# A new head: block 1's attention 8 half-slices earlier, raw weights in deeper flight, values loaded when a buffer is free

## The chip, the cores and the metric

The kernel runs on one core of one Trainium2 chip. The metric is the device time of that core in microseconds. Before the change the median of three runs is 1130.93 us (1129.2 to 1132.24).

The engines are named as the profile names them: PE is TensorE (PEld its weight loads), DVE is VectorE, ACT is ScalarE, POOL is GpSimd, and SP is SyncE, which here only issues DMAs. A q behind a name (SPq, ACTq) is that engine's sequencer.

## The reference

Three parts follow one another: windowed attention with sink tokens, a dense feed-forward layer with squared ReLU, and a mixture of eight experts of which each token takes one.

```python
# attention: q, k, v are (4, 8, 768, 64) float32; n_sink = 4, window = 128
scores = scale * np.matmul(q, k.transpose(0, 1, 3, 2))
keep = is_sink | in_window                 # key position < n_sink, or 0 <= row - key < window
scores = np.where(keep, scores, -1000000000.0)
a = softmax(scores)                        # with 1e-9 added to the sum
x = (a @ v) laid out as (3072 tokens, 512)
# dense layer: w_in (512, 2048), w_out (2048, 512), both float64
h = np.maximum(x @ w_in, 0.0);  x = (h * h @ w_out).astype(np.float32)
# experts: w_gate, w_output_gate (512, 8); w1 (8, 512, 1024); w2 (8, 1024, 512)
e_idx = argmax(x @ w_gate);  gate_w, eom = softmax weight, sigmoid of the output gate
out[token] = gate_w * eom * (np.maximum(x @ w1[e], 0.0) @ w2[e])
```

## The kernel before

The 3072 tokens are worked in 12 blocks of 256 (three to each of the four sequences). For a block t the attention makes its input x, then the dense layer runs over 16 units j of 128 hidden columns: `l1(t, j)` multiplies by a slice of w_in, applies ReLU and squares, and `l2` multiplies by a slice of w_out and adds up in PSUM, two units behind. The expert part comes after the twelfth block.

**Attention of a block.** Eight heads are taken as four pairs p, and a block's 256 rows as two halves n, which makes eight steps (p, n). `prep_k` and `prep_q` transpose k and q on TensorE; `scores` multiplies, applies the mask on VectorE (L528), exponentiates on ScalarE (L531) and normalises (L541, L543); `ptrans` transposes the probabilities (L560) and copies them (L564); `pv` multiplies by the values (L594) and copies out (L597). `attn_events` gives every such piece a due time in half-slices: a unit j of block t - 1 is two half-slices, and h0 is where block t's first scores are due. Events with a negative time lie in the head, ahead of the first unit of block 0. `loads` issues the DMAs of k, q and v for a block and a pair; `more`, called at the end of `prep_q`, loads two pairs ahead. Buffers are two for k and q, three for v.

**The weights.** w_in and w_out come as float64. They are converted on the chip in 32 pieces of 512 KB each, c = 2j for w_in's slice j and c = 2j + 1 for w_out's. `conv(c)` issues the raw load and returns `rest`, which does the work: two copies with a scale on ScalarE (L327, L330), two shift-and-or steps on VectorE (L334, L335) that give a float32 weight, and later `fin`, which splits it into a high part (L338, ScalarE) and a low part (L339, VectorE). Block 0 computes with the float32 weight itself, in TensorE's fp32 mode; all later blocks use the split parts. The first NBOOT = 3 raw pieces have buffers of their own (`braw`), the rest share three staging buffers (tag `stage`) with the set-up of the gate (`setup2`) and other short-lived tiles. `cstep(n)` does the next n pieces, with `fetch` loading ahead of them.

**What sets the order.** The program is written out by loops over half-slices: `for h in range(-46, 0)` is the head, with events, a conversion every third half-slice and the gate's set-up at h = -24; then come the units g = 16 t + j. A planner orders each engine's instructions ahead of the run from this written order, priorities (`tc.high_priority`) and estimated costs, and it may take an instruction early where its inputs and a buffer are there. `tc.keep_in_program_order` pins an instruction to the written order on its engine, and `behind(x, y)` puts x behind y on one engine without a semaphore. At run time every engine works in order, a DMA queue's issuing engine too, so a DMA that waits for a buffer holds what is behind it.

**Lines of the change.** The raw loads (L305 to L322), ScalarE's two copies (L327, L330), `loads` (L360), the q tiles (L439 to L443), `more` (L480), the end of `pv` (L596), `attn_events` (L647), the square in `l1` (L688), `cstep` (L897), the head (L919 to L948). `fill` (L105) puts small matmuls without a result between the head's others on TensorE.

Of the kernel before, what the change touches and what calls it, by code (L numbers as in the profile page):

```python
# [47 lines left out]
def kern(ctx, tc, q, k, v, n_sink, window, w_in, w_out, w_gate, w_og, w1, w2, out):  # L48
# [238 lines left out]

    fbuf = att.tile([128, 2, 512], F32, tag="PT", name="fbuf", bufs=1)

    fins, used = {}, {}  # L290

    def after(x, y):

# [11 lines left out]
    def conv(c):  # L305
        j, which = divmod(c, 2)
        if c < NBOOT:
            raw, dq = braw[c], A
        else:
            raw = cv.tile([128, 512, 2], I32, tag="stage", bufs=3, name="craw")  # L310
            dq = SY
        if which == 0:
            x = dq.dma_start(out=raw[:].rearrange("p (k f) w -> p k (f w)", k=4),
                         in_=w_in.bitcast(I32)[:, 256 * j:256 * j + 256].rearrange("(k p) f -> p k f", p=128))
            hi, lo = (WI[:, j, n].rearrange("p k f -> p (k f)") for n in range(2))
        else:
            x = dq.dma_start(out=raw[:].rearrange("p f w -> p (f w)"), in_=w_out.bitcast(I32)[128 * j:128 * j + 128, :])
            hi, lo = (WO[j // 8][:, j % 8, n] for n in range(2))
        if c < NBOOT + 2:
            tc.keep_in_program_order(x)  # L320
        if c < NBOOT:
            behind(x, brd[0])  # L322

        def rest():
            L, Hh = raw[:, :, 0], raw[:, :, 1]

            x = A.activation(out=Hh.bitcast(F32), in_=Hh.bitcast(F32), func=AF.Copy, scale=2.0 ** -112)  # L327
            if c < NBOOT:
                tc.keep_in_program_order(x)
            A.activation(out=L, in_=L.bitcast(U32), func=AF.Copy, scale=0.93 * 2.0 ** -29)  # L330
            n = NF * which + j
            f = fw[n] if n < len(fw) else fbuf[:, j % 2]
            fi = f.bitcast(I32)
            V.scalar_tensor_tensor(out=fi, in0=Hh, scalar=3, in1=L, op0=ALU.logical_shift_left, op1=ALU.bitwise_or)  # L334
            V.scalar_tensor_tensor(out=fi, in0=Hh, scalar=-2147483648, in1=fi, op0=ALU.bitwise_and, op1=ALU.bitwise_or)  # L335

            def fin():
                A.activation(out=hi, in_=f, func=AF.Copy)  # L338
                x = V.tensor_tensor(out=lo, in0=f, in1=hi.bitcast(F32), op=ALU.subtract)  # L339
                if n < len(fw):  # L340
                    after(x, used[n])

            if n < len(fw):
                fins[n] = fin
            else:
                fin()
        return rest
# [9 lines left out]
    moe.tile([128, HOME // 4], F32, name="gap1", bufs=1)  # L357
    xTs = {}

    def loads(t, p, kinds="kqvs"):  # L360
        b, u = divmod(t, NQ // 2)
        s0 = 256 * u
        for nm, src, m in (("k", k, 3), ("q", q, 2), ("v", v, 3)):
            if nm not in kinds:
                continue
            x = att.tile([128, m, 2, D], F32, tag=nm + "n", name=nm + "n", bufs=3 if nm == "v" else 2)
            lo = s0 - 128 * (m - 2)
            o = 0
            if lo < 0:
                lo, o = 0, 1  # L370
            nb = m - o
            for e in range(2):
                x_ = (A if t == 0 and (nm == "q" and p < 2 or nm == "v" and p == 0) else SY).dma_start(out=x[:, o:m, e, :],
                             in_=src[b, 2 * p + e, lo:lo + 128 * nb, :].rearrange("(n s) d -> s n d", s=128))
                if t == 0 and (p >= 2 or nm == "v"):
                    pin(x_)
                if brd and t == 0 and p < 3:
                    behind(x_, brd[0])
            nat[nm, t, p] = x
        if u == 0 and p == 0 and "s" in kinds:  # L380
            x = att.tile([H * NS, D], F32, tag="vs", name="vs", bufs=1)
            x_ = SY.dma_start(out=x[:], in_=v[b, :, 0:NS, :])
            if t == 0:
                pin(x_)
            nat["vs", b] = x
# [42 lines left out]
    def prep_q(t, p):  # L428
        x = nat.pop(("q", t, p))
        if t < T32:  # L430
            ps = psO.tile([128, 4, 128], F32, tag="O", name="psq")
        else:
            ps = psS.tile([128, 512], F32, tag="s0", name="psq")[:, 0:256].rearrange("p (n c) -> p n c", n=2)
        if t == 0:
            fill(ps[:].rearrange("p n c -> p (n c)"), 1)
        for n in range(2):
            PE.transpose(ps[:, n], x[:, n].rearrange("p h d -> p (h d)"), ident[:])
        if t < STK:
            own = t // T32  # L439
            if own not in qbuf:  # L440
                qbuf[own] = att.tile([128, 2, 2, 2, 128], F32R if own else F32, tag="qT", name=f"qT{own}", bufs=1)
            o = qbuf[own][:, p % 2]
            qTt[t, p] = o  # L443
        if t < T32:
            if p % 2:
                A.activation(out=o[:, 0], in_=ps[:, 0:2], func=AF.Copy)
            else:
                V.tensor_copy(out=o[:, 0], in_=ps[:, 0:2])
            Vt[t, p] = nat.pop(("v", t, p))
            more(t, p)  # L450
            return
        if t < STK:
            A.activation(out=o[:, 0], in_=ps[:, 0:2], func=AF.Copy)
            V.tensor_tensor(out=o[:, 1], in0=ps[:, 0:2], in1=o[:, 0].bitcast(F32), op=ALU.subtract)
        else:
            if "s" not in qbuf:
                o = qbuf["s"] = att.tile([128, 2, 2, 2, 128], F32R, tag="qT", name="qst", bufs=1)
                for e in range(2):
                    r = HALF[1 - e]
                    G.tensor_copy(out=o[r, 1, e].rearrange("p n (a c) -> p (n a) c", c=64),  # L460
                                  in_=ident[r, None, 64 * e:64 * e + 64].broadcast_to([64, 4, 64]))
            o = qbuf["s"]
            qTt[t, p] = o
            for e in range(2):
                A.activation(out=o[HALF[e], 0, e], in_=ps[HALF[e], 0:2], func=AF.Copy)
            for e in range(2):
                V.tensor_tensor(out=o[HALF[e], 1, e], in0=ps[HALF[e], 0:2], in1=o[HALF[e], 0, e].bitcast(F32), op=ALU.subtract)
            for e in range(2):
                G.tensor_copy(out=o[HALF[1 - e], 0, e], in_=o[HALF[e], 0, e].bitcast(F32))

        n0 = 1 if t % 3 == 0 else 0
        x = nat.pop(("v", t, p))
        o = att.tile([128, 3, 2, 2, D], F32R, tag="V", name="V", bufs=2)
        for e in range(2):
            G.tensor_copy(out=o[:, n0:3, e, e, :], in_=x[:, n0:3, e, :])
            G.tensor_tensor(out=o[:, n0:3, e, 1 - e, :], in0=x[:, n0:3, e, :], in1=o[:, n0:3, e, e, :].bitcast(F32), op=ALU.subtract)
        Vt[t, p] = o
        more(t, p)

    def more(t, p):  # L480
        tt, pp = (t, p + 2) if p + 2 < 4 else (t + 1, p - 2)
        if tt < NBLK:
            loads(tt, pp)

    def prep_sink(b):
        t = nat.pop(("vs", b))
# [14 lines left out]
    def scores(t, p, n):  # L501
# [26 lines left out]
                V.tensor_tensor_reduce(out=P[:, e, 0:W], in0=ps[e][:, 0:W], in1=mask[:, 0:W], scale=-SCALE, scalar=3.0e38,  # L528
                                       op0=ALU.add, op1=ALU.min, accum_out=st[:, e:e + 1])
        for e in range(2):  # L530
            A.activation(out=P[:, e, 0:W], in_=P[:, e, 0:W], func=AF.Exp, scale=-1.0, bias=st[:, e:e + 1],  # L531
                         accum_out=st[:, 4 + e:5 + e])
        V.tensor_scalar(out=st[:, 6:8], in0=st[:, 4:6], scalar1=1e-9, scalar2=None, op0=ALU.add)
        V.reciprocal(out=st[:, 6:8], in_=st[:, 6:8])  # L534
        if t >= T32 and i >= 2:
# [46 lines left out]
    def pv(t, p, n):  # L582
# [3 lines left out]
        if t < T32:  # L586
# [8 lines left out]
                              start=(kb == 0), stop=(kb == nk - 1))  # L595
            xo = xr if t else xT0  # L596
            A.activation(out=xo[:, p, 128 * n:128 * n + 128], in_=ps[:, 0:128], func=AF.Copy)  # L597
            return
        ps = psO.tile([128, 2, 2, 128], F32, tag="O", name="pso")
        for e in range(2):  # L600
# [46 lines left out]
    def attn_events(t):  # L647

        ev = []
        h0 = 32 * (t - 1) - 8  # L650
        a0, a1, a2, a3 = LEADS[min(t, 3)]
        for p in range(4):
            ev.append((h0 + 8 * p - a0, lambda p=p: prep_k(t, p)))
# [18 lines left out]
    def l1(t, j):  # L672
# [12 lines left out]
                PE.matmul(ps[:], lhsT=WI[:, j, a_, kk, :], rhs=x[:, b_, kk, :], start=(n == 0), stop=(n == 11))  # L685
        hq = moe.tile([128, 256], F32, tag="r", name="r", bufs=2)
        A.activation(out=hq[:], in_=ps[:], func=AF.Relu)  # L687
        E_ = G if t == 0 and j % 2 else V  # L688
        if t == 0 and NF + j < len(fw):
            o = moe.tile([128, 256], F32, tag="h2", name="h32", bufs=3, padded_shape=[128, 512])  # L690
            E_.tensor_tensor(out=o[:], in0=hq[:], in1=hq[:], op=ALU.mult)
# [205 lines left out]
    def cstep(n):  # L897
        for _ in range(n):
            if st_["done"] >= NC:
                return  # L900
            fetch(min(NC, st_["done"] + 2))
            rests.pop(st_["done"])()
            st_["done"] += 1

# [16 lines left out]
    loads(0, 2, "q")  # L921
    loads(0, 1, "v")
    loads(0, 0, "s")
    fetch(NBOOT)
    events = sorted((e for t in range(NBLK) for e in attn_events(t)), key=lambda e: e[0])
    events.reverse()

    def run_to(h):
        while events and events[-1][0] <= h:
            h_, f = events.pop()  # L930
            with (tc.high_priority(200) if h_ < 0 else ExitStack()):
                f()

    def gate_events(t):
        g = gate_pieces(t)
        h0 = 32 * (t + 1)
        for o, f in zip((4, 8, 12, 16) if t == NBLK - 2 else (6, 14, 22, 30), g):
            events.append((h0 + o, f))
        events.sort(key=lambda e: -e[0])

    for h in range(-46, 0):
# [2 lines left out]
            masks(wide, 1)  # L944
        if h == -24:
            setup2()
        if h >= -39 and h % 3 == 0:
            cstep(1)  # L948
    bootS.close()
    wpool2 = ctx.enter_context(tc.tile_pool(name="wpool2", bufs=1))  # L950
# [314 lines left out]
```

## Time and profile before

| view | value |
|---|---|
| profiled execution, its own time | 1127.99 us |
| its span, first to last instruction | 1126.2 us |
| mean granted TensorE clock | 0.998 |
| PE busy | 1101.4 us (98%), 6858 matmul instructions |
| PEld busy | 937.3 us (83%) |
| DVE busy | 778.6 us (69%) |
| ACT busy | 667.1 us (59%) |
| POOL busy | 443.9 us (39%) |
| HBM read and written | 85.82 and 13.76 MB |

The busy shares are means over the whole span. The table of 40 slices on the profile's page shows that the first four or five slices of 28 us differ from the rest: DVE 4, 7, 8, 9, 8 tenths and the core's DMA engines 6, 6, 7, 7, 2 tenths, against 1 or 2 tenths of DMA in the slices that follow. PE's time is that of modelled matmuls that overlap, so a busy PE is not one at its peak. Stretches of the trace are told in us from the start of the span.

### The profile page before, as it was taken

To read this page: it belongs to the slowest core of one execution; us is meant where nothing else is said; L and a number is where in the kernel's file an instruction comes from. 1 tells how busy PE (TensorE), PEld (TensorE's weight loads), DVE (VectorE), ACT (ScalarE), POOL (GpSimd) and SP (SyncE) were. 2 spreads that over 40 slices of the span, in tenths; PEclk is the share of its full clock that TensorE was granted. 3 is DMA by queue.
4 is the path that set the end of the run, shared out by engine and by line. 5 is a ranking of instruction groups with operands and counts; after the bars stand their busy time and mean duration, and the time that the engine had idled before them with its cause. 6 is when DMAs were issued, how large, how long until landed. Compare 5 with 4: busy or idle time off the path is not lost. (4 is left out here: it accounts for less than half of the span.)

```text
span 1126.2 us, 23923 instructions
## 1 busy us (share of the span) xinstructions
PE 1101.4 (98%) x6858; PEld 937.3 (83%) x6858; DVE 778.6 (69%) x2102; ACT 667.1 (59%) x1821; POOL 443.9 (39%) x989
## 2 busy tenths in 40 slices
PE   8999999999999999999999999999999999999997
PEld 4556788988999989999989999997788888888886
DVE  4789877788887778887878787567412566864144
ACT  5888877877787878787878787464222222222200
POOL 2313564346675437675336665210211222211121
PEclk9999999999999999999999999999999999999999
DMA  6677202111211111211112110395411456654111
GB/s 157 172 229 223 59 21 51 40 52 37 56 29 50 36 48 39 57 29 47 33 39 56 41 32 2 55 235 160 132 40 48 154 186 227 214 201 147 49 46 34
DMA packets 140416, 100.34 MB, mean 89 GB/s; under 512 B 104931, under 2 KB 113251, under 8 KB 140262
## 3 DMA queue, kind: packets, MB, share of 16 engines
q1 hardware_dynamic: 132020, 82.41, 26.1%
q0 software_dynamic: 5408, 14.19, 3.7%
q10 hardware_dynamic: 2834, 1.97, 0.6%
q8 instruction: 63, 1.03, 0.4%
q14 instruction: 91, 0.75, 0.3%
HBM read 85.82 MB, written 13.76 MB: 88 GB/s over the span
## 5 line engine op out<-in xcount | busy, mean ns | idle before, releaser
L685 PE MATMUL psh<-xT,WI 128*128 128x256 f32 x2112 | 283.5, 283 | 0.0
L685 PEld LDWEIGHTS psh<-xT,WI 128*128 128x128 f32 x2112 | 265.6, 188 | 7.7 <-issue 0.5
L1027 PE MATMUL psh<-WI,xt 128*128 (+1 forms) x672 | 162.1, 395 | 1.0 <-ACT xt L1007 0.7
L709 PE MATMUL psx<-WOb,h 128*128 128x512 f32 x576 | 150.0, 397 | 0.9 <-ACT h L696 0.4
L1027 PEld LDWEIGHTS psh<-WI,xt 128*128 128x128 f32 x672 | 123.8, 188 | 26.7 <-ACT xt L1007 1.4
L709 PE MATMUL psx<-WOa,h 128*128 128x512 f32 x528 | 138.7, 397 | 0.0
L694 DVE TENSOR_TENSOR r<-r 128x256 f32<-128x256 f32 x180 | 91.5, 509 | 56.8 <-ACT r L687 55.4
L1043 DVE TENSOR_TENSOR ht<-psht,ht 128x512 fp32r<-128x512 f32 x56 | 38.5, 689 | 121.1 <-ACT ht L1007 120.7
L709 PEld LDWEIGHTS psx<-WOb,h 128*128 128x128 f32 x576 | 101.9, 188 | 20.3 <-ACT h L696 2.1
L696 ACT ACTIVATE h<-r 128x256 fp32r<-128x256 f32 x184 | 76.3, 415 | 58.2 <-DVE r L694 54.3
L709 PEld LDWEIGHTS psx<-WOa,h 128*128 128x128 f32 x528 | 92.8, 188 | 15.2
L1065 POOL DMA_INDIRECT out_dram<-xg,pidx x28 | 28.4, 1016 | 189.1 <-ACT xg L1064 139.2
L697 DVE TENSOR_TENSOR h<-r,h 128x256 fp32r<-128x256 f32 x184 | 83.2, 452 | 23.5 <-ACT h L696 20.9
L576 POOL TENSOR_SCALAR_AFFINE_SELECT PT<-PT 128x256 fp32r<-128x256 f32 x224 | 98.0, 471 | 2.7 <-DVE PT L572 2.7
L531 ACT ACTIVATE P<-P,st 128x260 f32<-128x260 f32 (+1 forms) x192 | 92.5, 485 | 7.2 <-DVE st L528 3.6
L687 ACT ACTIVATE r<-psh 128x256 f32<-128x256 f32 x192 | 72.9, 380 | 34.9 <-PE psh L685 30.0
L1033 ACT ACTIVATE r<-psh 128x512 f32<-128x512 f32 x48 | 28.7, 599 | 98.5 <-PE psh L1027 96.7
L1056 PE MATMUL psy<-WOb,ht 128*128 (+1 forms) x336 | 84.0, 398 | 0.0
L612 POOL TENSOR_TENSOR xr<-tB,tC 128x128 f32<-128x128 f32 x80 | 37.9, 473 | 114.0 <-DVE tB L611 71.9
L1056 PE MATMUL psy<-WOa,ht 128*128 (+1 forms) x336 | 82.2, 392 | 0.0
L998 POOL DMA_INDIRECT xg<-x2tab,pidx x30 | 40.3, 1343 | 94.5 <-issue 51.6
L543 ACT ACTIVATE P<-P,st 128x132 f32<-128x132 f32 (+2 forms) x168 | 62.3, 415 | 20.5 <-DVE st L534 17.7
(460 smaller groups left out, 2106.6 us busy)
## 6 DMA issues: line engine op xcount, KB each, us to landing
raw<-in_moe_w_dram SPq DMA_DIRECT2D x36, 1024.0 KB
craw<-in_moe_w_out_dram SPq DMA_DIRECT2D x15, 512.0 KB
craw<-in_moe_w_in_dram SPq DMA_DIRECT2D x14, 512.0 KB
x2tab<-x2s SPq DMA_DIRECT2D x24, 256.5 KB
kn<-in_k_dram SPq DMA_DIRECT2D x64, 96.0 KB
vn<-in_v_dram SPq DMA_DIRECT2D x64, 96.0 KB
qn<-in_q_dram SPq DMA_DIRECT2D x94, 64.0 KB
kn<-in_k_dram SPq DMA_DIRECT2D x34, 64.0 KB
```

Of the source, the lines that this page charges most:

```text
L531: A.activation(out=P[:, e, 0:W], in_=P[:, e, 0:W], func=AF.Exp, scale=-1.0, bias=st[:, e:e + 1], accum_out=st[:, 4 + e:5 + e])
L543: A.activation(out=P[:, e, 0:W], in_=P[:, e, 0:W], func=AF.Copy, scale=st[:, 6 + e:7 + e])
L576: G.affine_select(out=both[:, 1 - b, e], in_=bf[:, 0, e], pattern=[[0, 2], [1 - 2 * b, 128]], compare_op=ALU.is_gt if b else ALU.is_ge, fi ...
L685: PE.matmul(ps[:], lhsT=WI[:, j, a_, kk, :], rhs=x[:, b_, kk, :], start=(n == 0), stop=(n == 11))
L687: A.activation(out=hq[:], in_=ps[:], func=AF.Relu)
L694: E_.tensor_tensor(out=hq[:], in0=hq[:], in1=hq[:], op=ALU.mult)
L696: A.activation(out=o[:, 0], in_=hq[:], func=AF.Copy)
L697: V.tensor_tensor(out=o[:, 1], in0=hq[:], in1=o[:, 0].bitcast(F32), op=ALU.subtract)
L709: PE.matmul(acc[t][m][:], lhsT=o[:, a_, 128 * m:128 * m + 128], rhs=WO[j // 8][:, j % 8, b_, :], start=(j == 0 and n == 0), stop=(j == NF ...
L998: G.indirect_dma_start(out=x, out_offset=None, in_=x2tab[:] if s >= PRE else x2tab[0:256 * (NBLK - 3)], in_offset=bass.IndirectOffsetOnAxi ...
L1027: PE.matmul(ps[:], lhsT=o[:, a_, kk, :], rhs=wview(n, par + 2048 * b_ + 512 * kk, 512), start=(c == 0), stop=(c == 11))
L1056: PE.matmul(yp[s][:], lhsT=o[:, a_, kk, :], rhs=wview(2 + n, par + 2048 * b_ + 512 * kk, 512), start=(n == 0 and kk == 0 and c == 0), stop ...
```

## The change

The diff does the following. Raw pieces 1 and 2 are issued by SyncE rather than ScalarE. Six raw pieces are issued before the loop of the head instead of three, and later the load runs three pieces ahead of the conversion instead of two. ScalarE's two copies of the first three pieces are put behind the exponential written last before them. `loads` leaves out what was loaded already. For pairs (0, 3) to (2, 2) values are no longer loaded by `more` but at the end of the `pv` step that reads the buffer last. The q tiles of blocks 0 and 1 lie in separate halves of their buffer. Block 1's attention is due 8 half-slices earlier, its steps no longer have the raised priority that negative times had, and the head does 12 conversions instead of 13. All squares of block 0 go to GpSimd instead of every second one.

```diff
@@ conv
-            raw, dq = braw[c], A
+            raw, dq = braw[c], A if c == 0 else SY
...
             if c < NBOOT:
-                tc.keep_in_program_order(x)
-            A.activation(out=L, in_=L.bitcast(U32), func=AF.Copy, scale=0.93 * 2.0 ** -29)
+                behind(tc.keep_in_program_order(x), exps[-1])
+            x = A.activation(out=L, in_=L.bitcast(U32), func=AF.Copy, scale=0.93 * 2.0 ** -29)
+            if c < NBOOT:
+                behind(x, exps[-1])
@@ loads
+    got, vnext = set(), [2]
...
-            if nm not in kinds:
+            if nm not in kinds or (nm, t, p) in got:
                 continue
+            got.add((nm, t, p))
@@ prep_q
-            o = qbuf[own][:, p % 2]
+            o = qbuf[own][:, p % 2, t if t < T32 else 0:]
@@ more
-            loads(tt, pp)
+            loads(tt, pp, "kqs" if 3 <= 4 * tt + pp <= 4 * T32 + 2 else "kqvs")
@@ scores
-            A.activation(out=P[:, e, 0:W], in_=P[:, e, 0:W], func=AF.Exp, scale=-1.0, bias=st[:, e:e + 1],
-                         accum_out=st[:, 4 + e:5 + e])
+            exps.append(A.activation(out=P[:, e, 0:W], in_=P[:, e, 0:W], func=AF.Exp, scale=-1.0, bias=st[:, e:e + 1],
+                         accum_out=st[:, 4 + e:5 + e]))
@@ pv, blocks 0 and 1
+            if n:
+                vnext[0] += 1
+                loads(*divmod(vnext[0], 4), "v")
@@ attn_events
-        h0 = 32 * (t - 1) - 8
+        h0 = 32 * (t - 1) - (16 if t == 1 else 8)
@@ l1
-        E_ = G if t == 0 and j % 2 else V
+        E_ = G if t == 0 else V
@@ cstep
-            fetch(min(NC, st_["done"] + 2))
+            fetch(min(NC, st_["done"] + 3))
@@ head
-    fetch(NBOOT)
+    fetch(NBOOT + 3)
...
-            with (tc.high_priority(200) if h_ < 0 else ExitStack()):
+            with (tc.high_priority(200) if t_ == 0 else ExitStack()):
...
-        if h >= -39 and h % 3 == 0:
+        if h >= -36 and h % 3 == 0:
             cstep(1)
```

## Rows read from the trace of the kernel before

**Rows 1.** Stages: stretch, its length, busy PE, PEld, DVE, ACT, POOL, clock, DMA.
```profile
5.00:21.00 16.00, 12.06 (x68) 6.57 (x67) 7.94 (x38) 6.74 (x25) 5.01 (x30) 0.92 0.68 181
21.00:43.00 22.00, 21.77 (x125) 12.24 (x124) 16.35 (x60) 19.52 (x57) 3.64 (x17) 0.98 0.58 153
43.00:60.00 17.00, 17.00 (x77) 10.24 (x76) 12.48 (x35) 13.13 (x32) 6.34 (x16) 1.00 0.67 194
60.00:125.00 65.00, 61.75 (x290) 39.54 (x289) 60.09 (x133) 57.37 (x133) 20.35 (x39) 1.00 0.68 203
...
150.00:775.00 625.00, 620.33 (x4460) 564.75 (x4459) 486.64 (x1550) 468.21 (x1379) 323.24 (x786) 1.00 0.23 55
```

**Rows 2.** Timeline of TensorE: start, us, line, out<-in, count, idle before and its releaser.
```profile
12.98 0.38 PE L105 MATMUL pspt<-idle 128*128 128x512 bf16 x1 [1.08 <-ACT PT L564]
...
14.33 0.66 PE L560 MATMUL pspt<-ident,P 128*128 128x128 f32 x4
17.66 0.41 PE L437 MATMUL psq<-ident,qn 128*128 128x128 f32 x2 [2.67 <-DMA qn<-in_q_dram]
...
22.85 0.27 PE L437 MATMUL psq<-ident,qn 128*128 128x128 f32 x1
...
42.65 1.89 PE L677 MATMUL psh<-xT,fw 128*128 128x256 f32 x8
...
121.72 1.99 PE L677 MATMUL psh<-xT,fw 128*128 128x256 f32 x8
...
125.11 1.18 PE L685 MATMUL psh<-xT,WI 128*128 128x256 f32 x8
```

**Rows 3.** TensorE by 1 us stretches: length, busy, granted clock, DMA share, GB/s.
```profile
19.00:20.00 1.00, 1.00 (x5) 0.50 0.53 120
20.00:21.00 1.00, 1.00 (x7) 0.50 0.07 11
```

**Rows 4.** Timeline of ScalarE and its queue, 7 to 13 us.
```profile
7.51 0.69 ACTq L317 DMA_DIRECT2D braw<-in_moe_w_out_dram  x1
8.26 0.40 ACT L531 ACTIVATE P<-P,st 128x128 f32<-128x128 f32 x1 [3.38 <-DMA vn<-in_v_dram]
...
12.54 0.38 ACT L564 ACTIVATE PT<-pspt 128x256 f32<-128x256 f32 x1 [1.72 <-DMA qn<-in_q_dram]
```

**Rows 5.** Timeline of SyncE's queue: DMA issues.
```profile
7.54 0.88 SPq L373 DMA_DIRECT2D qn<-in_q_dram  x2
...
13.90 0.92 SPq L373 DMA_DIRECT2D qn<-in_q_dram  x2
...
30.32 0.44 SPq L317 DMA_DIRECT2D craw<-in_moe_w_out_dram  x1
...
44.64 0.44 SPq L313 DMA_DIRECT2D craw<-in_moe_w_in_dram  x1
...
53.53 0.34 SPq L317 DMA_DIRECT2D craw<-in_moe_w_out_dram  x1
...
112.47 0.34 SPq L317 DMA_DIRECT2D craw<-in_moe_w_out_dram  x1
```

**Rows 6.** Timeline of VectorE: one conversion's second shift-and-or.
```profile
52.77 0.69 DVE L335 SCALAR_TENSOR_TENSOR fw<-craw,fw 128x512 int32<-128x512 int32 x1
```

**Rows 7.** DMA queues of 7 to 18 us: packets, MB, share (q10 ScalarE's, q1 SyncE's).
```profile
q10 hardware_dynamic: 1744, 1.70, 49.4%
q1 hardware_dynamic: 3602, 0.87, 36.8%
```

**Rows 8.** Timeline of GpSimd and VectorE: squares, and a conversion beside one.
```profile
45.38 0.42 DVE L691 TENSOR_TENSOR h<-r 128x256 f32<-128x256 f32 x1
...
84.14 1.05 POOL L691 TENSOR_TENSOR h<-r 128x256 f32<-128x256 f32 x1 [3.21 <-PE psx L706]
84.64 1.10 DVE L335 SCALAR_TENSOR_TENSOR fw<-craw,fw 128x512 int32<-128x512 int32 x1
```

**Rows 9.** Waits of SyncE's queue, 40 to 113 us: total, times, longest.
```profile
SPq L373 <- PE pso L594: 4.3, 2, 2.2
```

More of the change, by code (lines that the diff above doesn't have):

```diff
@@ L288, in kern @@
     fbuf = att.tile([128, 2, 512], F32, tag="PT", name="fbuf", bufs=1)
-    fins, used = {}, {}
+    fins, used, exps = {}, {}, []
     def after(x, y):
@@ L923, in kern @@
     loads(0, 0, "s")
-    fetch(NBOOT)
-    events = sorted((e for t in range(NBLK) for e in attn_events(t)), key=lambda e: e[0])
+    fetch(NBOOT + 3)
+    events = sorted(((h_, f_, t) for t in range(NBLK) for h_, f_ in attn_events(t)), key=lambda e: e[0])
     events.reverse()
@@ L929, in run_to @@
         while events and events[-1][0] <= h:
-            h_, f = events.pop()
-            with (tc.high_priority(200) if h_ < 0 else ExitStack()):
+            h_, f, t_ = events.pop()
+            with (tc.high_priority(200) if t_ == 0 else ExitStack()):
                 f()
@@ L937, in gate_events @@
         for o, f in zip((4, 8, 12, 16) if t == NBLK - 2 else (6, 14, 22, 30), g):
-            events.append((h0 + o, f))
+            events.append((h0 + o, f, t))
         events.sort(key=lambda e: -e[0])
```

## The prediction

> **What bounds the kernel now.** I read the clock and spans first (one core, granted clock 0.998 over the span), then the busy times by stage [rows 1]. TensorE is busy 620.33 of 625 us between 150 and 775 us, and there the change alters no work. Before that the other engines set the pace: in 60 to 125 us VectorE is busy 60.09 and ScalarE 57.37 of 65 us. In 5 to 21 us nobody is full: VectorE 7.94, ScalarE 6.74 of 16 us. So the head, up to the first matmul of block 1 at 125.11 us [rows 2], is the only place where this change can win or lose, and since TensorE is nearly full behind it, what the head gains goes nearly whole to the end.
>
> Inside the head the timeline of TensorE [rows 2] gives four marks. The q transposes of head pair 2 stand at 17.66 us after an idle of 2.67 us, ended by a load. Block 0's first layer starts at 42.65. Its last unit starts at 121.72, and block 1 follows at 125.11. What paces 42.65 to 121.72 is the conversion of the 32 weight pieces: the first-layer unit j needs piece 2j. The issue rows of SyncE [rows 5] and the second shift-and-or of VectorE [rows 6] show how: L335 starts at 52.77, lasts 0.69 and ends at 53.46; the next raw load is issued at 53.53. Piece 6 is issued at 44.64 and piece 31 at 112.47: 67.83 us over 25 gaps, 2.71 us each. With three staging buffers that is 8.1 us for a buffer's round of load, ScalarE and VectorE.
>
> **The change part by part.**
>
> *A. The first 21 us.* Three things go.
> First, raw pieces 1 and 2 leave ScalarE's queue. The issue at 7.51 takes 0.69 and ends at 8.20, and the first exponential starts at 8.26. The second stood behind a wait, in front of the copy at 12.54, which idled 1.72 us [rows 4]; TensorE idled 1.08 for that copy [rows 2].
> Second, k and q of pair 2 were loaded twice: q at 7.54 and again at 13.90 [rows 5], since the first preparation step asks for all kinds of a pair that was already loaded, and the second copy is the one used. Now each is loaded once. TensorE had finished its earlier work at 14.99 (14.33 + 0.66); less 1.1 it would come to those transposes at 13.9, so 17.66 - 13.9 = 3.8 us go.
> Third, after that idle the granted clock is 0.50, the 1.2 GHz level, from 19 to 21 us, with TensorE busy throughout [rows 3]. At the upper level the matmuls of these 2 us take 1; without the idle I take 0.7 us more, an estimate, since part of that time is latency. Sum 4.5 us: pair 3, whose q is transposed at 22.85 [rows 2], would be due at 18.3.
>
> What is late next are pair 3's loads. They are pinned behind pieces 1 to 4 on SyncE's queue now. By the DMA rows of 7 to 18 us [rows 7], 1.70 MB of raw pieces and one value pair took 49.4% of 11 us, 1.68 us for a 0.524 MB piece; 0.87 MB of q, k, v took 36.8%, 0.61 us for a pair of loads. From 7 us on stand pieces 0 to 4 (8.4) and the pairs v0, k2, q2, v1, v2, k3, q3 (4.3): 12.7 us, at the 0.866 busy share of those rows 14.7 us, so pair 3 lands at 21.7 us; at a full share at 19.7, with piece 5 also ahead at 23.6. Against 18.3 this gives back 3.4 (1.4 to 5.3). The attention of block 0 so wins 1.1 us (-0.8 to 3.1).
>
> The Trainium skill, "DMA: Bandwidth & Descriptors", section "Queues, rings and completion order", says that each DMA engine takes turns between the queues that have work, and takes each queue's own work in order. By that rule the old raw pieces on ScalarE's queue shared the engines with SyncE's small loads, and the new ones stand whole in front of pair 3; no run here shows it yet. The sum by it is the 21.7 us above, and without it (equal turns for all) about 19.7.
>
> The waiting is not lost: pieces 1 to 5 are on the chip then, and conversions that filled ScalarE in 21 to 43 us (19.52 of 22 busy) can run in its 9.26 idle us before. I take a third, 2.9 us; bounds 0 and 5 (not all the idle falls where a piece is ready). The new order edges only say that the first three pieces come behind the latest exponential; I cost them at nothing, covered by that idle, and at up to 1 us if they hold a piece. A: 4.0 us, from -0.8 to 8.1.
>
> *B. The hole at 43 to 60 us.* Between pieces 5 and 6 no raw load is issued from 30.32 to 44.64 [rows 5]: the gate's set-up takes one of the three staging buffers and its loads stand in the queue ahead of piece 6. So VectorE idles 4.52 and ScalarE 3.87 us in 43 to 60 [rows 1]. With pieces 3 to 5 loaded from some 10 us on instead of up to 30, their buffers come free while attention still fills the engines. I take 2.0 us, about half of the smaller idle; bounds 0 (the set-up still takes its buffer) and 4.5 (all of VectorE's idle).
>
> *C. The loop.* "Three ahead" in the code: I cost it at nothing, because the old loads were already issued within 0.1 us of a buffer's release (53.46 and 53.53). If the planner puts piece loads ahead of k, q, v loads the cost is a round's third, 2.7 us, covered by loads that are two pairs ahead. Value loads stood in SyncE's queue waiting for the second matmul step to free their buffer, 4.3 us in two waits [rows 9], and raw loads behind them went out late. They are issued behind the freeing step now. A delay of one buffer is shared by three, 4.3 / 3 = 1.4, and not each piece is the one waited for: I take 1.0 us (0 to 4.3). Separate q halves and loading nothing twice in the loop save no time that I can see.
>
> *D. Squares.* Eight squares of block 0 go from VectorE (0.42 us, [rows 8]) to GpSimd; on VectorE that frees 8 x 0.42 = 3.4 us. But beside GpSimd's square at 84.14, itself 1.05 us long, VectorE's L335 lasts 1.10 instead of 0.69 [rows 6, 8]: 0.41 us given back. Five of the eight old GpSimd squares stretched a VectorE instruction so: 5 x 0.41 = 2.1. Net 1.3 on VectorE, at its 92% share and with a longer chain from ReLU to second layer (0.6 us more, two units of slack): I take 0.5 (-1.5 to 2.7; below nothing where the stretched one is the L335 that TensorE waits for).
>
> The Trainium skill, "SBUF — State Buffer", section "Who interferes with whom", says that VectorE's instructions with two SBUF inputs and GpSimd's reads share a port pair as an exclusive lock. The 1.10 beside 1.05 us agrees. By it alone all eight would give back 0.41 and D would be 0.1 us.
>
> *E. Block 1's attention, 8 half-slices earlier,* moves two of its eight steps ahead of 42.65 us and the rest forward. Block 1's input can be split only when block 0's last first-layer unit is done (121.72 to 123.7 us, same buffer), so at the seam nothing is won directly; ScalarE and VectorE have less to do in the last 20 us and more in 21 to 60. Nothing in the middle; -2 (it delays block 0's start, ScalarE being 89% busy there) to +2. Dropping the priority of these steps and one piece more at j = 0 go the same way.
>
> Sum: 4.0 + 2.0 + 1.0 + 0.5 = 7.5 us; I round to 7 for parts that overlap (A's filled idle is partly B's). The profiled execution took 1127.99 us (span 1126.2): 1121.0. The median before is 1130.93, 2.94 above that execution: 1124.0 us.
>
> **The rivals.**
> 1. *Much more.* If conversions fill the early idle wherever they can, ScalarE's idle of 23 us in 5 to 125 (9.26 + 2.48 + 3.87 + 7.63) could halve: 12 us, 1119. For it: all six pieces are there by 24 us. Against: chains of exponential, transpose and copy remain. Chance 0.16.
> 2. *No change.* The round of a staging buffer stays 8.1 us, the set-up still takes a buffer, pair 3 comes late: 1 to 2 us, 1129.5. For it: nothing in the loop adds a buffer. Against: [rows 1] shows room in the first 60 us. Chance 0.15.
> 3. *The squares' lock.* Each moved square stretches an L335 on the path: 8 x 0.41 = 3.3 us on TensorE's wait, and half of the 7 is gone: 1130.93 - (7 - 0.5 - 3.3) = 1127.7. For it: [rows 8]. Against: GpSimd and VectorE meet only five times in eight. Chance 0.06.
> 4. *Slower.* The order on ScalarE is fixed before the run. If conversions of pieces 1 to 5 stand ahead of block 0's exponentials and a piece lands later than planned, ScalarE waits at the piece with all attention behind it. Place: 10 to 30 us. Price: 1.94 us (1.68 / 0.866) for each piece that comes late, and pair 3 late besides; five pieces and pair 3's 5.3 make 15 us against gains of 4.5 + 2 + 1 + 0.5 = 8, slower by 7: 1138. It decides from about 8 us of such waits. For it: the DMA engines stay nearly full until 22 us. Against: the order edges put the first three behind exponentials. Chance 0.11.
>
> **How the numbers follow.** The forecast (4 to 10 us less) has 0.52. Faster by over 0.3% (3.4 us, about what a measurement can tell): 0.52 + 0.16 = 0.68. Within: 0.15 + 0.06 = 0.21. Slower: 0.11. The forecast's own range is 1121 to 1127; with the rivals, 1115 (1 with all of A and B) to 1132.
>
> **What would show it.** A: q of pair 2 transposed before 15 us, no stretch at clock 0.50 near 20 us, first layer of block 0 at about 39 us. B: piece 6 loaded before 40 us and no break in the conversions. C: rounds near 8 us still. D: stretched L335s, near 1.1 us, about twice as many. The seam at about 118 us, and equal lengths behind it. Wrong: a seam at 125 or later, or ScalarE idling on raw pieces before 30 us.

## The result, and the profile after

The changed kernel takes 1140.54 us, the median of seven runs (1136.04 to 1147.42), beside 1130.93 us before (seven runs, 1129.2 to 1132.9) on the same chip: 1.0103 of the time, with a 95% interval of 1.0087 to 1.0120. It is slower by 1.0%, and the forecast was 1124.0. Its profiled execution took 1144.52 us (span 1142.8, mean granted clock 0.981), 16.5 more than that of before. It is one of the longer of its seven, and the one of before (1127.99) is below all of its seven, so the marks below place 16.5 us where the medians differ by 9.6.

Three marks place the 16.5. The first matmul of block 0's first layer moved from 42.7 to 58.5 us (15.8 more); from there to the first matmul of block 1 it takes 87.9 in place of 82.4 us (5.5 more); what lies behind takes 996.4 in place of 1001.1, mostly by less idle (TensorE is busy 983.6 us there, for 985.0). So most of the loss lies ahead of block 0's first unit. The stages after, with the columns of [rows 1]:

```profile
5.00:21.00 16.00, 14.70 (x84) 8.22 (x83) 11.14 (x47) 10.85 (x34) 5.52 (x31) 1.00 0.81 245
21.00:43.00 22.00, 18.52 (x79) 9.42 (x79) 11.94 (x39) 13.78 (x39) 4.22 (x19) 0.67 0.52 126
43.00:60.00 17.00, 13.34 (x51) 7.95 (x50) 10.57 (x34) 13.83 (x35) 0.79 (x5) 0.50 0.55 159
60.00:125.00 65.00, 60.10 (x264) 38.18 (x263) 55.26 (x109) 49.27 (x111) 29.80 (x45) 0.95 0.65 185
165.00:790.00 625.00, 621.47 (x4463) 565.58 (x4462) 486.51 (x1550) 468.71 (x1380) 322.25 (x787) 1.00 0.23 55
```

The first stage is better than before: more conversions, VectorE 11.14 for 7.94, ScalarE 10.85 for 6.74, and no low clock. The second has fewer instructions on every engine but GpSimd (TensorE 79 for 125, ScalarE 39 for 57), at clock 0.67, and the third runs at 0.50. VectorE, ScalarE and GpSimd, less busy than before over the two stages together, wait for others; TensorE has holes, and from 30 to 45 us it is nearly full (14.48 of 15 us, below), but at half speed. So this begins as a chain, not with a full engine. The last row is the steady part, 621.47 of 625 beside 620.33. TensorE's timeline shows where it begins, with the marks of [rows 2]:

```profile
12.40 0.28 PE L442 MATMUL psq<-ident,qn 128*128 128x128 f32 x1
...
24.27 0.41 PE L442 MATMUL psq<-ident,qn 128*128 128x128 f32 x2
25.93 0.49 PE L521 MATMUL pss<-kT,qT 64*128 64x128 f32 x4 [1.25 <-ACT qT L451]
...
26.80 0.55 PE L402 MATMUL psk__882<-ident,kn 128*128 128x128 f32 x3
...
29.29 1.01 PE L105 MATMUL pspt<-idle 128*128 128x512 bf16 x2 [1.73 <-DVE kT L407]
...
58.47 2.07 PE L685 MATMUL psh<-xT,fw 128*128 128x256 f32 x4
...
146.42 1.76 PE L693 MATMUL psh<-xT,WI 128*128 128x256 f32 x13
```

q of pair 2 is transposed from 12.40 us on (its second half at 15.02) and no longer at 17.66; pair 3's at 24.27. Then, at 26.80, three k blocks are transposed at once: three blocks are block 1's (block 0 has two). They take the tile that k transposes and probability transposes share (the pool `psT` has one buffer), so block 0's next probability transpose has to wait until VectorE has copied block 1's k out, 1.73 us. Why that copy is late stands on VectorE's timeline: conversions (L336, L337) run ahead of it. ScalarE's (the view of [rows 4]) shows the same for the hole of 1.25 us before: block 0's q copy (L451, at 25.52), for transposes that end at 24.68, stands behind a conversion (L330):

```profile
26.37 0.69 DVE L337 SCALAR_TENSOR_TENSOR fw<-craw,fw 128x512 int32<-128x512 int32 x1
27.08 0.69 DVE L336 SCALAR_TENSOR_TENSOR fw<-craw 128x512 int32<-128x512 int32 x1
27.80 0.69 DVE L337 SCALAR_TENSOR_TENSOR fw<-craw,fw 128x512 int32<-128x512 int32 x1
...
28.68 0.55 DVE L407 COPY kT<-psk__882 128x384 f32<-128x384 f32 x1
```

```profile
24.98 0.64 ACT L330 ACTIVATE craw<-craw 128x512 int32<-128x512 uint32 x1
25.52 0.36 ACT L451 ACTIVATE qT<-psq 128x256 f32<-128x256 f32 x1
25.78 0.67 ACT L327 ACTIVATE craw<-craw 128x512 f32<-128x512 f32 x1
26.35 0.69 ACT L330 ACTIVATE craw<-craw 128x512 int32<-128x512 uint32 x1
26.94 0.68 ACT L327 ACTIVATE craw<-craw 128x512 f32<-128x512 f32 x1
27.52 0.66 ACT L330 ACTIVATE craw<-craw 128x512 int32<-128x512 uint32 x1
28.08 1.13 ACT L340 ACTIVATE WI<-fw 128x512 fp32r<-128x512 f32 x2
...
30.76 0.38 ACT L569 ACTIVATE PT<-pspt 128x256 f32<-128x256 f32 x1 [0.51 <-PE pspt L565]
```

From 25.78 to 30.25 us ScalarE runs conversions in one piece, with no step of block 0 among them: they fill a gap, for the probability copy at 30.76 waits 0.51 us for TensorE and not for them. TensorE's holes of 1.25 and 1.73 us are followed by the low level of its clock, which [rows 3] showed before for two microseconds (stretch, length, busy, clock, DMA share, GB/s):

```profile
26.00:28.00 2.00, 1.56 (x13) 1.00 0.69 156
28.00:30.00 2.00, 0.71 (x2) 0.66 0.70 175
30.00:45.00 15.00, 14.48 (x48) 0.50 0.52 135
45.00:60.00 15.00, 11.38 (x42) 0.50 0.49 143
60.00:62.00 2.00, 2.00 (x9) 0.50 0.00 0
62.00:64.00 2.00, 2.00 (x14) 0.81 0.00 0
```

In 26 to 30 us TensorE was busy 2.27 of 4 us and the clock fell to 0.50, the 1.2 GHz level. It rose behind 62 us, after a stretch in which TensorE was busy throughout; but from 32 to 43 us TensorE is busy throughout as well, and the clock stayed at 0.50, so the trace doesn't tell what lets it rise. The queue of SyncE shows what that delay does to the loads (compare [rows 5, 9]):

```profile
30.23 0.45 SPq L313 DMA_DIRECT2D craw<-in_moe_w_in_dram  x1
...
56.38 7.57 SPq L378 DMA_DIRECT2D vn<-in_v_dram  x3
64.05 0.43 SPq L313 DMA_DIRECT2D craw<-in_moe_w_in_dram  x1
```

Piece 6 is issued at 30.23 and no longer at 44.64, but at 56.38 value loads, now issued behind the step that frees their buffer, hold the queue for 7.57 us, 6.2 of it in a wait for that step's matmul (pso L599), and the raw piece behind them with it. The last place is at 96 to 111 us, on GpSimd (compare [rows 8]):

```profile
102.31 4.80 POOL L551 CAST psk<-P 128x8 fp32r<-128x8 f32 x1 [2.35 <-DVE P L546]
107.05 0.19 POOL L552 CAST psk<-P 128x8 fp32r<-128x8 f32 x1
```

Two casts of the same 128x8 shape: one took 0.19 us, the other 4.80. While it lasted VectorE ran eight shift-and-or and subtract steps of 0.68 us one behind the other, each with two inputs in SBUF. The Trainium skill, "SBUF — State Buffer", section "Who interferes with whom", says that such an instruction and a GpSimd instruction that reads SBUF exclude each other; the trace agrees (the cast ends at 107.11 us, the last of the eight at 107.06), and shows that the wait can go on through several of them. By the waits of 95 to 112 us TensorE waited 3.1 us for the step behind that cast.

### The profile page after: what moved, and what is told of

The parts are those of the page before. It is cut to its first block, busy times and chain, and to the rows that moved or that the text cites. A ratio compares the mean times of both kernels' runs of the same rounds, so it can differ in the third digit from the quotient of the medians.

```text
span 1142.8 us, 23908 instructions
## 1 busy us (share of the span) xinstructions
PE 1113.9 (97%) x6858; PEld 945.2 (83%) x6858; DVE 779.8 (68%) x2094; ACT 667.5 (58%) x1821; POOL 450.7 (39%) x997
## 5 line engine op out<-in xcount | busy, mean ns | idle before, releaser
L717 PE MATMUL psx<-WOb,h 128*128 128x512 f32 x576 | 150.8, 398 | 0.8 <-ACT h L704 0.5
L717 PE MATMUL psx<-WOa,h 128*128 128x512 f32 x528 | 138.3, 397 | 0.0
L702 DVE TENSOR_TENSOR r<-r 128x256 f32<-128x256 f32 x176 | 88.9, 505 | 59.1 <-ACT r L695 57.7
L717 PEld LDWEIGHTS psx<-WOb,h 128*128 128x128 f32 x576 | 102.1, 188 | 20.0 <-ACT h L704 1.4
L717 PEld LDWEIGHTS psx<-WOa,h 128*128 128x128 f32 x528 | 92.9, 188 | 15.1
L705 DVE TENSOR_TENSOR h<-r,h 128x256 fp32r<-128x256 f32 x184 | 86.3, 469 | 23.5 <-ACT h L704 21.2
L533 DVE CUSTOM_DVE_ANT_0 P<-pss,M 128x260 f32<-128x260 f32 (+1 forms) x184 | 68.3, 398 | 17.4 <-PE pspt L565 4.6
```

Source lines behind the costliest of these rows:

```text
L702: E_.tensor_tensor(out=hq[:], in0=hq[:], in1=hq[:], op=ALU.mult)
L705: V.tensor_tensor(out=o[:, 1], in0=hq[:], in1=o[:, 0].bitcast(F32), op=ALU.subtract)
L717: PE.matmul(acc[t][m][:], lhsT=o[:, a_, 128 * m:128 * m + 128], rhs=WO[j // 8][:, j % 8, b_, :], start=(j == 0 and n == 0), stop=(j == NF ...
```

## The experiments

Theory 1: the early raw pieces bring conversions in front of block 0's attention (rival 4 of the prediction). Theory 2: block 1's attention, moved forward, takes engines and the one shared transpose buffer from block 0's last steps. Theory 3: the squares on GpSimd hold the loop. All ratios are to the kernel before, on the same chip, and are of medians. The marks (us of block 0's and of block 1's first matmul) are those of one profiled execution each; the mean clock is over its span.

| kernel | ratio, 95% interval | first unit | block 1 | clock |
|---|---|---|---|---|
| before | 1 | 42.7 | 125.1 | 0.998 |
| the change | 1.0103 (1.0087 to 1.0120) | 58.5 | 146.4 | 0.981 |
| raw loads as before | 1.0086 (1.0057 to 1.0116) | 53.6 | 135.8 | 0.992 |
| attention as before | 0.9981 (0.9965 to 0.9997) | 39.1 | 128.4 | 0.995 |
| squares as before | 1.0061 (1.0034 to 1.0088) | 58.6 | 139.9 | 0.986 |
| head filled | 1.0084 (1.0064 to 1.0104) | 53.0 | 136.2 | 0.999 |
| attention and squares as before | 1.0003 (0.9991 to 1.0016) | 38.8 | 128.3 | 0.993 |
| before + attention | 1.0069 (1.0047 to 1.0092) | 53.7 | 133.0 | 0.996 |
| before + squares | 1.0028 (1.0015 to 1.0041) | 43.7 | 127.2 | 0.993 |
| attention behind block 0's | 0.9975 (0.9963 to 0.9987) | 37.5 | 124.1 | 0.998 |
| the same, squares as before | 0.9957 (0.9942 to 0.9972) | 37.5 | 122.1 | 0.999 |
| before + attention behind | 1.0010 (0.9997 to 1.0023) | 41.9 | 125.8 | 0.993 |
| attention behind, raw loads as before | 1.0026 (1.0008 to 1.0044) | 40.2 | 131.8 | 0.991 |
| attention behind by 4, squares as before | 0.9947 (0.9930 to 0.9963) | 37.4 | 120.3 | 0.997 |

**One part undone.** Three kernels, each the change with one part taken back. The raw loads:

```diff
-            raw, dq = braw[c], A if c == 0 else SY
+            raw, dq = braw[c], A
-            fetch(min(NC, st_["done"] + 3))
+            fetch(min(NC, st_["done"] + 2))
-    fetch(NBOOT + 3)
+    fetch(NBOOT)
-        if h >= -36 and h % 3 == 0:
+        if h >= -39 and h % 3 == 0:
```

> The changed kernel with the raw loads as before (pieces 0 to 2 on ScalarE's queue, three at once, two ahead, 13 conversions in the head); all else as changed. Theory 1 (early conversions stand in front of block 0's attention on ScalarE and VectorE, TensorE idles at 24.7 to 29.3 us, its granted clock falls to 0.50 until 62 us): the conversions come later, no long stretch at 0.50, first unit of block 0 by 45 us instead of 58.5, 1128 to 1133 us. Theory 2 (block 1's attention moved forward takes the buffers and engines of block 0's): the stretch at 0.50 stays, 1137 to 1144 us. Theory 3 (all squares on GpSimd hold the loop): 1136 to 1141 us.

Measured 1.0086: theory 1 falls as the main cause. The first unit is still at 53.6 us without any early piece. That is 4.9 us sooner than the change's 58.5, with the clock at 1.00 in 21 to 43 us and 0.80 in 43 to 60, so the early pieces may have a part in the change's low clock; the intervals of the two ratios overlap. The attention's due time:

```diff
-        h0 = 32 * (t - 1) - (16 if t == 1 else 8)
+        h0 = 32 * (t - 1) - 8
```

> The changed kernel with block 1's attention at its old due time (8 half-slices later). Theory 1: little changes, clock at 0.50 for some 30 us, 1137 to 1144 us. Theory 2 (block 1's k transposes at 26.8 us take the one PSUM bank that block 0's probability transposes need, and wait for a copy behind conversions on VectorE): the hole of TensorE at 27.6 to 29.3 us goes and the clock holds, 1128 to 1133 us. Theory 3: 1136 to 1141 us.

Measured 0.9981: with this line alone taken back the loss is gone. The first unit stands at 39.1 us, where the prediction had put it (about 39), and the clock stays up in the very stretch that was at 0.67. The first row gives the first layer's matmuls with the starts of the first and the last, the next two the stages:

```profile
L685 PE MATMUL psh<-xT,fw x128: 378/379/483, 39.1 to 115.0; 128*128 128x256 f32 x128
```

```profile
21.00:43.00 22.00, 18.63 (x121) 11.65 (x122) 17.48 (x60) 21.02 (x60) 3.98 (x20) 1.00 0.68 167
43.00:60.00 17.00, 16.70 (x89) 10.69 (x88) 15.46 (x35) 15.92 (x39) 5.01 (x11) 1.00 0.86 246
```

The early conversions are all in it (ScalarE 21.02 of 22 us, for 13.78 in the change), so they do no harm where block 1's attention is due as before. The squares:

```diff
-        E_ = G if t == 0 else V
+        E_ = G if t == 0 and j % 2 else V
```

> The changed kernel with every second square of block 0 on VectorE again. Theories 1 and 2: the first 60 us are the same with the clock at 0.50, 1136 to 1143 us, at most 3 us below the changed kernel. Theory 3 (the squares on GpSimd stretch VectorE's instructions and delay GpSimd's other work, as in TensorE's wait of 3.07 us for a GpSimd step at 104 to 107 us): 1130 to 1136 us.

Measured 1.0061: perhaps a part of the loss (block 0 is 81.3 us long in place of 87.9; the intervals of the ratios just touch), none of it ahead of the first unit, 58.6.

**The clock.** Is the low clock the cost, or its sign? Eight matmuls without a result behind each group of k and q transposes, in block 0 and block 1's first two pairs, keep TensorE busy in the head:

```diff
+    def hold(y):
+        o = psH.tile([128, 256], F32, tag="h", name="psh")
+        for _ in range(8):
+            behind(PE.matmul(o[:], lhsT=idle[:], rhs=..., start=True, stop=True), y)
...
+        if t == 0 or t == 1 and p < 2:
+            hold(y)
```

> The changed kernel with eight matmuls without a result (128 x 256, bf16) put behind every q and k transpose group of the head, so that TensorE has less idle there; nothing else is touched. If the clock is what makes the changed kernel slow: the granted clock stays at 1.00 or the stretch at 0.50 shortens below 10 us, 1131 to 1136 us (the line through the seven runs of mean clock and time gives 1134.5 at a mean clock of 0.998). If the order of the work is what costs and the clock only shows it: 1138 to 1146 us with the clock at 1.00.

Measured 1.0084. In the stages the clock is held at 1.00:

```profile
21.00:43.00 22.00, 22.00 (x164) 14.28 (x162) 15.58 (x50) 18.10 (x50) 4.62 (x19) 1.00 0.68 166
43.00:60.00 17.00, 14.43 (x95) 9.24 (x93) 14.97 (x47) 15.96 (x43) 6.60 (x18) 1.00 0.75 216
```

and yet the first unit stands at 53.0, 10.4 later than before, in the shortest of its six executions. The extra matmuls take time of TensorE too:

```profile
L396 PE MATMUL psh<-idle 128*128 128x256 bf16 x96 | 15.7, 273 | 0.0
```

So the 5.5 us that came back (58.5 less 53.0) are no upper bound on what the clock costs. Two kernels without these matmuls agree with the 53.0: the raw loads as before (53.6) and, below, the kernel before with the attention alone (53.7), both with the old raw loads and neither with the long stretch at 0.50; the two with that stretch, the change and the one with the squares as before, stand at 58.5 and 58.6. By these marks some ten us are the order and some five go with the low clock. The seven runs of the change point the same way: at mean clock 0.996 it still takes 1136.04 us, 5.1 more than before, and at 0.980 it takes 1147.42. The ratio of the filled head, 1.0064 to 1.0104, doesn't part from the change's.

**Are the parts additive, is the attention enough, what do the squares cost alone?** Four more kernels: the change with attention and squares taken back; the kernel before with the attention's line alone (priorities as before); the kernel before with the squares' line alone; and the change with block 1's steps due as early as in it, but written no earlier than half-slice -4, which puts all that were due sooner behind block 0's steps but for its last multiplication by the values (so the first of them are also written later, by up to 17 half-slices):

```diff
-        return ev
+        return [(max(h_, -4), f_) for h_, f_ in sorted(ev, key=lambda e: e[0])] if t == 1 else ev
```

> The changed kernel with two parts undone: block 1's attention at its old due time and every second square on VectorE. Theory 2 (block 1's steps, written among block 0's last ones, delay block 0's first unit) with theory 3 (the eight more squares on GpSimd block and are blocked by VectorE's two-input instructions, some 6 us on block 0's units): both costs go and the early loads stay, first unit at 39 to 41 us, block 1 at 120 to 124, 1123 to 1129 us, ratio to before 0.990 to 0.998. Rival (the two costs overlap, or what is gained ahead of block 0's units is given back in them): like the run with the attention alone undone, ratio 0.997 to 1.002.

> The kernel before with one part of the change: block 1's attention 8 half-slices earlier. Theory 2: it is enough by itself, first unit of block 0 at 48 us or later instead of 42.7, ratio 1.005 to 1.013. Rival (it costs only together with early raw pieces or without the raised priority, which its steps still have here): ratio 0.997 to 1.003.

> The kernel before with one part of the change: all squares of block 0 on GpSimd. Theory 3: block 0's units take 4 to 7 us longer (82.4 before), VectorE's instructions beside squares last near 1.1 us, ratio 1.002 to 1.006. Rival (the squares only hurt where block 1's attention crowds the same stretch): ratio 0.998 to 1.002.

> The changed kernel with the steps of block 1's attention still due 8 half-slices earlier, but none written before half-slice -4, so that they stand behind nearly all of block 0's attention. Theory 2 (the place in front of block 0's last steps costs, not the earliness): first unit of block 0 by 43 us and the clock at 1.00 there, ratio 1.000 to 1.005 (the squares' cost stays). Rival (the same work ahead of block 0's units costs wherever it stands): first unit at 50 us or later, ratio 1.007 to 1.012.

The attention alone costs 0.7% (1.0069, first unit 53.7 us) in a kernel with the old loads: it is enough by itself, and little low clock goes with it (0.93 in 21 to 43 us, 1.00 in 43 to 60). Of the 11.0 us at the first unit 7.9 are left at block 1 and 7.8 at the end; the rest may be work of block 1 that was only done sooner. Written behind block 0's steps it turns into a gain: 0.9975, first unit 37.5. So the place costs, and not the work: a step of block 1 that stands ahead of one of block 0 on an engine holds it, as the k transposes at 26.80 did. ScalarE's timeline of that kernel, at the place shown above, has block 0's copies and exponentials between the conversions again, the probability copy at 26.86 and no longer at 30.76:

```profile
26.03 0.68 ACT L327 ACTIVATE craw<-craw 128x512 f32<-128x512 f32 x1
26.59 0.39 ACT L451 ACTIVATE qT<-psq 128x256 f32<-128x256 f32 x1
26.86 0.40 ACT L569 ACTIVATE PT<-pspt 128x256 f32<-128x256 f32 x1
27.12 0.70 ACT L330 ACTIVATE craw<-craw 128x512 int32<-128x512 uint32 x1
27.68 0.72 ACT L327 ACTIVATE craw<-craw 128x512 f32<-128x512 f32 x1
28.24 0.44 ACT L536 ACTIVATE P<-P,st 128x128 f32<-128x128 f32 x1
```

The squares alone cost 0.28% (0.15 to 0.41), 3.2 us. In the profiled execution block 0 is only 1.1 us longer than before, not 4 to 7 as expected. The groups of GpSimd and the waits of TensorE point to the way: the cast of the sink probabilities took 952 ns in the mean, 470 before, and the sink's transpose on TensorE waits 2.5 us for it, where it waited 0.5 before (in each pair the first row is of before):

```profile
L546 POOL CAST psk<-P 128x8 fp32r<-128x8 f32 x9 | 4.2, 470 | 29.3 <-DVE P L541 26.9 <-DVE st L534 2.4
L546 POOL CAST psk<-P 128x8 fp32r<-128x8 f32 x9 | 8.6, 952 | 20.0 <-DVE P L541 17.1 <-DVE st L534 2.4 <-ACT P L543 0.4
```

```profile
PE psst L622 <- POOL psk L548: 0.5, 1, 0.5
PE psst L622 <- POOL psk L548: 2.5, 1, 2.5
```

With both undone the time is 1.0003, no better than with the attention alone undone, where 0.990 to 0.998 had been expected: a first unit that comes 3.9 us sooner gave nothing at the end. TensorE's timeline of that kernel at the seam shows where it went. L442, L565, L610 and L528 at this place are attention steps of block 2, the matmul with the wide inputs L717 is block 0's second layer:

```profile
113.25 0.59 PE L685 MATMUL psh<-xT,fw 128*128 128x256 f32 x2
...
119.50 2.57 PE L717 MATMUL psx<-WOb,h 128*128 128x512 f32 x10 [0.30 <-DVE h L705]
121.91 0.38 PE L442 MATMUL psq<-ident,qn 128*128 128x128 f32 x2
122.13 0.27 PE L565 MATMUL pspt<-ident,P 128*128 128x128 f32 x1
124.66 0.98 PE L610 MATMUL pso<-PT,V 128*128 128x256 f32 x4 [2.25 <-POOL PT L581]
...
128.34 2.06 PE L693 MATMUL psh<-xT,WI 128*128 128x256 f32 x8
```

The first layer's last matmul starts at 113.5 us in this kernel, 9.8 earlier than before (123.3), but the attention that should lie beside block 0's units hasn't kept up: it stands alone between the blocks, 6.3 us from the end of the second layer to block 1.

**The better version.** Four kernels on the version with block 1's steps written behind: squares taken back; the kernel before with only that attention (and these steps without the head's priority); the raw loads taken back (ScalarE's queue issues the first three of them again, not six as the expectation says); and the first of them due 4 earlier in place of 8.

> The changed kernel with block 1's attention steps written behind block 0's (as in the run before this one that was faster) and half of block 0's squares back on VectorE. Theory 2 (place in front of block 0's last steps costs; the squares cost beside it): the squares alone measured 0.0028 of the time, so this run takes 2 to 3 us off the 0.9975 of the kernel with all squares on GpSimd: 0.994 to 0.996, about 1124 to 1127 us, first unit of block 0 near 37.5 us and seam near 122. Rival (not additive, as when both were undone with block 1 at its old time): 0.997 to 0.999, seam near 124 as before.

> The kernel before, with block 1's attention due 8 half-slices earlier but written behind block 0's attention (and without block 0's priority), nothing else changed. Theory 2: it gives no loss: 0.997 to 1.001, first unit of block 0 near 42.7 us as before, seam 122 to 125. Rival (the earliness itself costs, by ScalarE's and VectorE's time in the loop): 1.003 to 1.006.

> The changed kernel with block 1's attention written behind block 0's, and the raw pieces loaded as before (first six by ScalarE's queue, two ahead). If the early raws are what brings the first unit forward (step A of the prediction): first unit at 41 to 43 us in place of 37.5, time 0.999 to 1.002. Rival (the early raws do nothing in sum, the loop takes up what the head gains): 0.996 to 0.999, like the same kernel with early raws.

> As the first of these four, with block 1's attention due 4 half-slices earlier than in the kernel before, in place of 8. If its earliness matters in the loop (block 0 is 89 us long with block 1 at its old time, 87 with it 8 earlier), the time lies between: 0.996 to 0.999, block 0 some 87 to 88 us long. Rival (4 is enough to fill the loop): the same as the first, 0.994 to 0.996.

The first gave 0.9957, in the range of theory 2, near its upper end, with the first unit and the seam where it had them. At its seam the same step of block 2 stands behind block 1's first matmul:

```profile
116.36 4.37 PE L717 MATMUL psx<-WOb,h 128*128 128x512 f32 x18
...
122.06 0.36 PE L693 MATMUL psh<-xT,WI 128*128 128x256 f32 x1
...
123.59 0.86 PE L610 MATMUL pso<-PT,V 128*128 128x256 f32 x4 [0.62 <-POOL PT L581]
```

The second gave 1.0010: earlier attention without the early loads wins nothing. The third gave 1.0026, a little above its range: beside 0.9975 for the same kernel with early loads, these are worth some 0.5%, about 6 us, and its first unit is at 40.2, 2.7 later (41 to 43 had been expected). The fourth gave 0.9947 (median 1126.5 us of ten runs): 4 half-slices are enough, as the rival had it; the intervals of the two overlap, and block 0 is 82.8 us long for 84.5. Both beat the kernel before and the change.

## Why the prediction was wrong

**E is the step that failed**: "Nothing in the middle; -2 (it delays block 0's start, ScalarE being 89% busy there) to +2." Alone it cost 0.69% (0.47 to 0.92), 7.8 us; in the change it makes the difference between 1.0103 and 0.9981, 13.8 us (0.0122 x 1130.93). The prediction named the mechanism and weighed it by ScalarE's share, as if the moved steps' busy time were the price. The price was a place in the queues: steps of block 1 in front of block 0's, a shared transpose buffer, conversions that ran ahead of the copies TensorE waited for, and a low clock that goes with some five of the 15.8 us at the first unit. It also said that "at the seam nothing is won directly"; with the early loads in, the block 1 that started at 128.3 us with the old due time (squares as before) started at 122.1 with the earlier due time in the right place.

**What bounds the kernel** held only by half. "What the head gains goes nearly whole to the end" failed where attention kept its old due time: 3.5 us at the first unit became 2.1 at the end (0.9981), and 3.9 became nothing (1.0003). Units of block 0 and attention steps are due against each other, and whoever shortens one finds the other late. The row that was read for VectorE and ScalarE as the pace of 60 to 125 us [rows 1] also has TensorE busy 61.75 of 65 us, more than either, and TensorE waited only 2.3 us for L335 there: the prediction didn't ask how much room TensorE left in that stretch.

**A's sum held, one of its terms didn't.** With E out of the way the first unit came at 39.1 (squares moved) and 38.8 us (squares as before), for a forecast of about 39; in the change q of pair 2 is transposed at 12.40 and 15.02, and there is no 0.50 stretch near 20 us. But pair 3 came at 24.27, later than the 22.85 of before and 0.7 past the upper of the bounds given (23.6), so the 1.1 us that block 0's attention was to win isn't there at that mark, and that the sum came out is luck as far as this term goes. Its load was issued at 16.98 and took 3.21 us to issue. No row gives a load as what ended TensorE's wait there, so this doesn't tell how much of the 24.27 is the loads' order. The early conversions did fill ScalarE's idle, 10.85 for 6.74 us in 5 to 21.

**B's mark held**, piece 6 at 30.23, before 40 us (its other half didn't: in the change ScalarE's two copies break off from 28.2 to 45.1 us). In the kernel with the attention as before VectorE is busy 15.46 of 17 us in 43 to 60, for 12.48, so the hole was filled; its 2.0 us can't be told from A's.

**C** is not settled by itself: in the change the value loads behind the freeing step waited longer in SyncE's queue than before, 9.0 us in four waits over 40 to 113 us, for 4.3 in two. No run took that part back alone.

**D had the wrong sign.** For +0.5 (bounds -1.5 to 2.7) the squares alone cost 3.2 us. The 0.41 us per stretched conversion was priced; there were eleven such rows of over 1 us in the changed kernel's head, for four before. Not priced was the other side of the lock: GpSimd's own sink casts, which wait while VectorE converts, and for which TensorE waits. The price depends on the order: taking the squares back gave 0.2 and 0.4% less in two kernels, with intervals that overlap or touch, and nothing in the one whose block 1 was held at the seam by attention.

**The rivals.** Rival 4 had the outcome (1138, chance 0.11), and conversions ahead of block 0's exponentials are in the trace; but its cause, raw pieces that come late, isn't: ScalarE never idles for one in 24 to 31 us, over 5 to 125 us such idle sums to 3.5 us, for 3.9 before, and without early pieces the loss stays. The prediction's own sign of being wrong, ScalarE idling on raw pieces before 30 us, shows 0.7 us; the other, a seam at 125 or later, came true. Rival 3's direction was right for the squares. The range ended at 1132 and left the outcome out.

## What to carry to other kernels

When a step is moved forward in a program whose engines work in order, ask first what it then stands in front of, on every engine and in every shared buffer, and only then how busy the engines are. Move it in due time, but write it behind the work that the end waits for. A gain in one of two interleaved streams of work reaches the end only when the other comes forward too: here the change without attention and squares (early loads and the rest, 1.0003) and the earlier attention behind block 0's, alone (1.0010), gave nothing, and both together 0.9957.

## What the runs showed of the hardware

A GpSimd cast of 128x8, 0.19 us when alone, took 4.80 us beside eight VectorE steps with two inputs. TensorE at half clock stayed there for some 32 us, from 30 to 62, with 14.48 of 15 and 11.38 of 15 us busy by its own (slower) time. It was busy throughout from 32 to 43 us without a rise, and throughout from 60 us on when the clock rose behind 62. The seven runs of the change go from 1136.04 us at mean clock 0.996 to 1147.42 at 0.980, where those of the kernel before beside them span 3.7 us (9.9 in 23 runs on another chip).
